# A gated mix of a state-space model and a feed-forward block: parameter rows on another queue, the decay from a tanh

## The chip, the cores and the metric

The kernel runs on one core of a Trainium2 chip. The metric is the device time of one execution in microseconds (us), less is better. A core has TensorE (PE, matrix products into PSUM banks), VectorE (DVE), ScalarE (ACT), GpSimd (POOL) and SyncE (SP), each with its own instruction stream in order, and 16 DMA engines that several queues feed. DMAs can be issued from the streams of SP, ScalarE and GpSimd.

## What is computed

```python
def _A_ref(x, ...):                       # state-space model, P = D = 640 complex states
    dt = exp(log_dt);  Lam_bar = exp(dt * Lam)          # Lam = Lambda_re + 1j * Lambda_im
    B_bar = ((Lam_bar - 1.0) / Lam)[:, None] * Bmat
    Bu = einsum("bld,pd->blp", x, B_bar)
    h_t = Lam_bar * h_{t-1} + Bu_t                      # over 2048 tokens
    return 2.0 * einsum("blp,dp->bld", h, Cmat).real + x * Dskip
def _B_ref(x, w1, b1, w2, b2):            # feed-forward, F = 1728
    return gelu_tanh(x @ w1 + b1) @ w2 + b2
g = sigmoid((x * gate_w).sum(-1, keepdims=True))
out = g * _A_ref(x) + (1 - g) * _B_ref(x)
```

x is 1 x 2048 x 640, all inputs and the output are bf16.

## The kernel before, in words

The 2048 tokens are cut into four chunks of 512, the 640 features and the 640 states into five tiles of 128, the 1728 hidden units into thirteen tiles of 128 and a last one of 64. For each chunk there are four stages: `ff1` (x times w1, a GELU on ScalarE), `ssm` (x times B on TensorE, copied to bf16 by ScalarE, then the recurrence on VectorE), `fin_b` (the hidden layer times w2) and `fin_a` (the states times C, added to a seed x * Dskip that VectorE writes into the PSUM bank, gated by VectorE into an output tile `ot` and stored).

The complex recurrence is done without complex multiplications inside the scan. With a decay r = exp(dt * Lambda_re) and an angle, VectorE multiplies Bu by tables of cosines and sines (TCOS, TSIN), runs two real scans with the factor r (line 497), and multiplies back (lines 482 to 521). The tables are made in the first 27 us: a matrix product with the identity (line 372) turns the parameter rows collected in `prmA` (log_dt, Lambda_im, Lambda_re; five rows of 128 each) into columns `colA`; ScalarE takes dt = exp(log_dt) (line 374) and r = exp(dt * Lambda_re) (line 378); VectorE makes the angles `u` for 64 positions and five special ones kept in `tf`, reduces them, and ScalarE takes sines and cosines (386, 388). VectorE then doubles the tables twice (`double`, lines 406 to 420), and lines 422 to 428 write the upper half. A second matrix of rows, `prmB` (gate_w and b1), is turned in the same way at line 391 into `colB`, which holds the GELU's biases.

The order on TensorE, VectorE and ScalarE is the order of the program: the lines from 195 on are scheduled by hand, with an estimate of each engine's clock (`ck`) that decides between which matmuls a VectorE step of the recurrence is let out (`let_out`, `dve_now`). The order on SP and GpSimd is that of the program too. The DMAs issued by SP and ScalarE take one of eight completion semaphores in turn; a DMA waits until the one eight places ahead of it has landed.

At the start, SP issues the first tokens (line 136), two transposing loads of the rest of chunk 0's features (`load_turned`, line 151), then weights; the tokens' first two feature tiles are turned on TensorE instead (`turn_first`). ScalarE's queue issues three of the w1 tiles and two parameter rows. GpSimd makes the identity, an index row and constants, and issues no DMA:

```python
    load_turned(0)
    rows(nc.sync, prmA[2 * KS:3 * KS, :], A_Lambda_re)
    rows(nc.scalar, prmA[0:KS, :], A_log_dt)
    rows(nc.scalar, prmA[KS:2 * KS, :], A_Lambda_im)
    load_turned(H)
```

TensorE meanwhile multiplies whatever has arrived: `part(kd, a)` takes feature tile kd of token tile a, `strip` several token tiles, for six hidden tiles in six banks. The turn of `prmA` stands between `part(0, 3)` and `part(1, 3)`, that of `prmB` after the third hidden tile of the last strip. On VectorE the copy of `colB` (line 392) stands ahead of everything that makes the tables out of the sines (418 on).

Later, `load_xn` loads the untransposed tokens of a chunk for the seeds; those of chunk 3 are loaded in halves, the others whole. Output tiles have two buffers, so the third waits for the first one's store.

Of the kernel before, what the change touches and what calls it, by code (L numbers as in the profile page):

```python
# [10 lines left out]
ALU = mybir.AluOpType  # L11
ACT = mybir.ActivationFunctionType
BF16 = mybir.dt.bfloat16
F32 = mybir.dt.float32
I32 = mybir.dt.int32

P = 128
T = 2048
D = 640
# [4 lines left out]
KS = D // P  # L24
KF = (F + P - 1) // P
F_LAST = F - (KF - 1) * P
NT = T // P
TPC = CH // P
H = TPC // 2
# [12 lines left out]
def kernel(  # L42
# [19 lines left out]
    nc = tc.nc  # L62
# [4 lines left out]
    const = ctx.enter_context(tc.tile_pool(name="const", bufs=1))  # L67
# [7 lines left out]
    def bank(dtype=F32):  # L75
        return ps.tile([P, CH * 4 // (4 if dtype == F32 else 2)], dtype, name="bank")
# [18 lines left out]
    ident = const.tile([P, P], BF16, name="ident")  # L95
    prmA = const.tile([P, P], BF16, name="prmA")
    NB = KS + KF - 1
    prmB = const.tile([P, P], BF16, name="prmB")
    colA = const.tile([P, 3 * KS], F32, name="colA")
    colB = const.tile([P, NB], F32, name="colB")  # L100
    Dbc = const.tile([P, D], BF16, name="Dbc")
    glast = const.tile([P, 2, KS], F32, name="glast")
    carry = const.tile([P, 2, KS], F32, name="carry")
# [9 lines left out]

    ldt_c = colA[:, 0:KS]
    lim_c = colA[:, KS:2 * KS]
    lre_c = colA[:, 2 * KS:3 * KS]
    b1_c = colB[:, KS:NB]


    def load_xn(c, a0=0, a1=TPC, queue=None):  # L120
        if a0 == 0:
            xn[c] = xnp.tile([P, TPC, D], BF16, name="xn")
        r0 = c * CH + a0 * P
        (queue or nc.sync).dma_start(out=xn[c][:, a0:a1, :], in_=x2d[r0:r0 + (a1 - a0) * P, :].rearrange("(a p) d -> p a d", p=P))
# [4 lines left out]
    def rows(queue, dst, v):  # L129
        queue.dma_start(out=dst, in_=v.rearrange("(j p) -> j p", p=P))  # L130

    KA = 2
    xn[0] = xnp.tile([P, TPC, D], BF16, name="xn")

    def load_x0(queue, a0, a1, d0, d1):
        queue.dma_start(out=xn[0][:, a0:a1, d0:d1], in_=x2d[a0 * P:a1 * P, d0:d1].rearrange("(a p) d -> p a d", p=P))
# [13 lines left out]
    def load_turned(a):  # L150
        nc.sync.dma_start_transpose(out=xT[0][:, KA:KD, a * P:(a + H) * P], in_=x2d[a * P:(a + H) * P, KA * P:D])

    load_turned(0)
    rows(nc.sync, prmA[2 * KS:3 * KS, :], A_Lambda_re)
    rows(nc.scalar, prmA[0:KS, :], A_log_dt)
    rows(nc.scalar, prmA[KS:2 * KS, :], A_Lambda_im)
    load_turned(H)
    load_w1a(nc.sync, 4)
    load_w1a(nc.sync, 3)
    for kd in range(KD):  # L160
        if kd == 1:
            rows(nc.sync, prmB[KS:NB, :], B_b1[0:(KF - 1) * P])
            rows(nc.sync, prmB[0:KS, :], gate_w)
        nc.sync.dma_start(out=w1b[kd][:], in_=B_w1[kd * P:(kd + 1) * P, cut1:cut2])
    for t, k0, k1 in ((w1c_lo, 0, 3), (w1c_hi, 3, KD)):
        nc.sync.dma_start(out=t[:, :, 0:F - cut2], in_=B_w1[k0 * P:k1 * P, cut2:F].rearrange("(k p) f -> p k f", p=P))
# [1 line left out]
    HC = CH // 8  # L168
    tfi = work.tile([P, HC], I32, name="e")
    nc.gpsimd.iota(tfi[:], pattern=[[1, HC]], base=0, channel_multiplier=0)  # L170
    nc.gpsimd.memset(b1x[:, F_LAST:F_LAST + 1], 0.0)
    NQ = 5
    NP = NQ + HC
# [7 lines left out]
    nc.sync.dma_start_transpose(out=xT[1][:], in_=x2d[CH:2 * CH, :])  # L181
    nc.sync.dma_start_transpose(out=CT_re[:], in_=A_C_re[:, :])
    nc.sync.dma_start_transpose(out=CT_im[:], in_=A_C_im[:, :])
    for k0, k1 in ((0, KF - 1),):
        nc.sync.dma_start(out=w2_sb[:, k0:k1, :], in_=B_w2[k0 * P:k1 * P, :].rearrange("(kf p) d -> p kf d", p=P))
    for h in range(2):
        nc.sync.dma_start(out=w2l[h * F_LAST:(h + 1) * F_LAST, :], in_=B_w2[(KF - 1) * P:F, :])
    load_x0(nc.sync, 0, TPC, KA * P, D)
    nc.sync.dma_start(out=b2bc[:], in_=B_b2.rearrange("(o d) -> o d", o=1).to_broadcast([P, D]))
    nc.sync.dma_start(out=Dbc[:], in_=A_Dskip.rearrange("(o d) -> o d", o=1).to_broadcast([P, D]))  # L190
    nc.sync.dma_start_transpose(out=xT[2][:], in_=x2d[2 * CH:3 * CH, :])
    nc.sync.dma_start_transpose(out=xT[3][:], in_=x2d[3 * CH:4 * CH, :])
    load_xn(1)

    ctx.enter_context(tc.manual_schedule(engines={E.PE, E.DVE, E.Activation}))

# [1 line left out]
    class Clock:  # L198
        pe = 3.4
        act = 12.0  # L200
# [26 lines left out]
    def act(cost):  # L227
        ck.act = max(ck.act, ck.pe + 0.2) + cost
        return ck.act
# [5 lines left out]
    pA = bank()  # L235
# [24 lines left out]
    def col(name, dtype=F32, n=KS):  # L260
        return const.tile([P, n], dtype, name=name)

    dt16 = col("dt16", BF16)
    dtl = col("dtl")
    limp = col("limp")
    thp_c = col("thp_c")
    r_c = col("r_c")
    hs = [None] * NCH
    gel = [None] * NCH
    gbs = [None] * NT  # L270
    def ff1_mm(p, c, kf, kd, t0=0, t1=CH, first=None, last=KD - 1):
        w, f0 = (w1a, 0) if kf < FA else (w1b, FA) if kf < FB else (w1c, FB)
        w = w[kd][:, (kf - f0) * P:(kf - f0 + 1) * P]
        nc.tensor.matmul(p[:, t0:t1], lhsT=w, rhs=xT[c][:, kd, t0:t1],  # L274
                         start=(kd == 0) if first is None else first, stop=(kd == last), skip_group_check=first is not None)
        pe(t1 - t0)

    def ff1_act(p, c, kf):
        nc.scalar.activation(out=gel[c][:, kf, :], in_=p[:, :], func=ACT.Gelu_apprx_tanh, bias=b1_c[:, kf:kf + 1])  # L279
        act(0.69)  # L280
# [71 lines left out]
    def over(c, n):  # L352
        return c.rearrange("p (k o) -> p k o", o=1).to_broadcast([P, KS, n])
# [15 lines left out]
    part(1, 2)  # L369
    part(0, 3)  # L370
    pP = bank()
    nc.tensor.matmul(pP[:, 0:3 * KS], lhsT=prmA[:], rhs=ident[:, 0:3 * KS], start=True, stop=True, skip_group_check=True)
    nc.vector.tensor_copy(out=colA[:], in_=pP[:, 0:3 * KS])
    nc.scalar.activation(out=dt16[:], in_=ldt_c, func=ACT.Exp)
    nc.vector.tensor_scalar(out=limp[:], in0=lim_c, scalar1=INV_2PI, scalar2=None, op0=ALU.mult)
    nc.vector.tensor_tensor(out=dtl[:], in0=dt16[:], in1=lre_c, op=ALU.mult)
    nc.vector.tensor_tensor(out=thp_c[:], in0=dt16[:], in1=limp[:], op=ALU.mult)
    nc.scalar.activation(out=r_c[:], in_=dtl[:], func=ACT.Exp)
    nc.vector.tensor_tensor(out=u, in0=tf[:].rearrange("p (o i) -> p o i", o=1).to_broadcast([P, KS, NP]), in1=over(thp_c[:], NP), op=ALU.mult)
    part(1, 3)  # L380
    strip(2, 0, HT, False)
# [6 lines left out]
    nc.scalar.activation(out=FSC[:, KS:2 * KS, 0:NP], in_=ab, func=ACT.Sin, scale=-TWO_PI_M, bias=halfpi[:])  # L388
    for kf in range(FA):
        if kf == 3:  # L390
            nc.tensor.matmul(pA[:, 0:NB], lhsT=prmB[:], rhs=ident[:, 0:NB], start=True, stop=True, skip_group_check=True)
            nc.vector.tensor_copy(out=colB[:], in_=pA[:, 0:NB])
        ff1_mm(banks[kf], 0, kf, 3, 0, CH, False, 3)
    for kf in range(FA):
        ff1_act(banks[kf], 0, kf)
# [3 lines left out]
            ff1_mm(two_banks[i], 0, FA + i, kd)  # L399
    for i in range(2):  # L400
        ff1_act(two_banks[i], 0, FA + i)
    for t, k0, k1 in ((w1c_lo, 0, 3), (w1c_hi, 3, KD)):
        nc.gpsimd.tensor_copy(out=t[:, :, n1c - 1:n1c], in_=colB[:, k0:k1].rearrange("p (k o) -> p k o", o=1))
    ff1(0, FA + 2)

    def double(n, i):
        lo, hi = slice(0, n), slice(n, 2 * n)
        s, c = (over(t[:, i * KS:(i + 1) * KS], n) for t in (sq, cq))
        m1, m2 = (scr[:, (3 + j) * KS * P:(3 + j) * KS * P + KS * n].rearrange("p (k i) -> p k i", k=KS) for j in range(2))
        nc.vector.tensor_tensor(out=m1, in0=FC[:, :, lo], in1=c, op=ALU.mult)  # L410
        nc.vector.tensor_tensor(out=m2, in0=FS[:, :, lo], in1=s, op=ALU.mult)
        nc.vector.tensor_tensor(out=FC[:, :, hi], in0=m1, in1=m2, op=ALU.subtract)
        nc.vector.tensor_tensor(out=m1, in0=FC[:, :, lo], in1=s, op=ALU.mult)
        nc.vector.tensor_tensor(out=m2, in0=FS[:, :, lo], in1=c, op=ALU.mult)
        nc.vector.tensor_tensor(out=FS[:, :, hi], in0=m1, in1=m2, op=ALU.add)
# [3 lines left out]
    double(HC, 4)  # L419
    double(2 * HC, 3)  # L420
    nsH = col("nsH")
    nc.vector.tensor_scalar(out=nsH[:], in0=sH, scalar1=-1.0, scalar2=None, op0=ALU.mult)
    for ks in range(KS):
        for dst, X, xs, Y in ((TCOS, FS, nsH, FC), (TSIN, FC, sH, FS)):
# [109 lines left out]
    def ssm(c, at={}):  # L534
        hs[c] = hsp.tile([P, 2 * KS, CH], BF16, name="hs")
        for ks in range(KS):
            if ks in at:
                at[ks]()
            bu = work.tile([P, 2, CH], BF16, name="bu", bufs=8)
            for ri, BT in enumerate((BT_re, BT_im)):  # L540
                p = bank()
                for kd in range(KD):
                    nc.tensor.matmul(p[:], lhsT=BT[ks >= KSA][:, kd, (ks % KSA if ks < KSA else ks - KSA) * P:][:, 0:P], rhs=xT[c][:, kd, :],  # L543
                                     start=(kd == 0), stop=(kd == KD - 1))
                    pe(CH)
                nc.scalar.activation(out=bu[:, ri, :], in_=p[:], func=ACT.Identity)  # L546
                act(0.6)
            scan_ops(c, ks, bu, ck.act)
            if c == 0 and ks == 0:
                later(0, 1.6, factors)  # L550
            let_out(ck.pe)
# [43 lines left out]
    def first_banks(c):  # L595
        biased(c, "wide", 0)
        biased(c, "wide", 1)
# [90 lines left out]
    ff1(2, 0, {1: lambda: fold(3), 4: lambda: fold(4), 9: lambda: seed(0), 11: lambda: seed(1)})  # L688
    gates(2)
    fin_a(0)  # L690
    load_xn(2)
    ssm(2, {KS - 1: lambda: first_banks(1)})
    fin_b(1, seeds(1))
    fin_a(1)
# [41 lines left out]
```

## Time and profile before

| what | value |
|---|---|
| median of 5 runs | 216.05 us (215.59 to 216.78) |
| the profiled execution | 216.31 us, its span 214.5 us |
| granted TensorE clock | 1.00 |
| busy: TensorE, VectorE, ScalarE, GpSimd | 209.1, 188.0, 101.9, 1.8 us |
| DMA | 16.23 MB, mean 76 GB/s |
| idle of TensorE until prmA had landed | 0.5 us |

The span runs from the first instruction to the end of the last. Busy times of engines overlap. In a row of waits, the name on the left waited for the one on the right; in a chain, each piece was released by the one before it. L372 is line 372 of the kernel. The page's slices show how the loads lie: the DMA engines are busy in the first quarter of the span, and little after that.

```profile
DMA  6898999999200000061000006100000000110012
```

Each digit is the busy share in tenths of one of 40 slices of 5.4 us.

### The profile page before, as it was taken

The numbers are of one execution on the slowest core, as the hardware profiler recorded it, in microseconds if no ns is written. First come the engines' busy times: TensorE is split into PE (matmuls) and PEld (weight loads), VectorE is DVE, ScalarE is ACT, GpSimd is POOL, SyncE is SP. The second block draws the span as 40 slices with busy tenths as digits, with TensorE's granted clock in tenths as the row PEclk, the third lists the DMA queues.
The fourth block names the chain that finished last, engine by engine and source line by source line (L and its number), as shares of the span: only waits on it lengthen the run. The fifth ranks groups of instructions, "written<-read, shape, count | busy, mean of one in ns | idle before, by whom it ended". The sixth has DMA issues, their size and how long they took to land.

```text
span 214.5 us, 3528 instructions
## 1 busy us (share of the span) xinstructions
PE 209.1 (97%) x1372; PEld 125.1 (58%) x1383; DVE 188.0 (88%) x381; ACT 101.9 (47%) x182; POOL 1.8 (1%) x15
## 2 busy tenths in 40 slices
PE   8899999999999999999999999999999989999994
PEld 5745444454576644774456777444457567676773
DVE  2589999999989999998999999799999999995153
ACT  3599856665868588203653210456691421405100
POOL 1001000000000000000000000000000000000000
PEclk9999999999999999999999999999999999999999
DMA  6898999999200000061000006100000000110012
GB/s 185 208 172 184 226 176 219 355 248 200 67 0 0 3 0 0 14 184 63 0 0 3 0 0 176 42 29 0 2 5 12 0 3 0 61 64 0 0 63 64
DMA packets 33139, 16.23 MB, mean 76 GB/s; under 512 B 24546, under 2 KB 33122, under 8 KB 33122
## 3 DMA queue, kind: packets, MB, share of 16 engines
q1 hardware_dynamic: 32526, 15.38, 30.6%
q10 hardware_dynamic: 596, 0.63, 0.9%
q8 instruction: 11, 0.18, 0.4%
q14 instruction: 6, 0.05, 0.1%
HBM read 7.48 MB, written 2.62 MB: 47 GB/s over the span
## 4 chain that ended last, share of the span: by engine, by line
DVE 70%; PE 20%; DMA 5%; issue 2%; ACT 1%; ACTq 0%; DVEq 0%
DVE g L497 19%; PE bank L661 10%; DVE wa L478 10%; DVE wb L478 10%; PE bank L602 7%; DVE v L478 6%; DVE hs L478 6%; DMA out_dram<-ot 4%; DVE bank L576 3%; DVE ot L666 3%; PE bank L274 2%; DVE CT_re L466 2%; DVE CT_im L466 2%; DMA prmA<-in_A_Lambda_im_dram 1%; DVE g L426 1%
## 5 line engine op out<-in xcount | busy, mean ns | idle before, releaser
L602 PE MATMUL bank<-w_sb,gel 128*128 128x384 bf16 (+1 forms) x416 | 57.9, 299 | 0.0
L602 PEld LDWEIGHTS <-gel 128*128 128x128 bf16 x416 | 40.3, 98 | 17.0 <-issue 0.8
L546 ACT ACTIVATE bu<-bank 128x512 bf16<-128x512 f32 x40 | 23.6, 597 | 37.3 <-PE bank L543 37.2
L279 ACT ACTIVATE gel<-bank,colB 128x512 bf16<-128x512 f32 x52 | 33.9, 692 | 11.1 <-PE bank L274 10.8
L661 PEld LDWEIGHTS <-hs 128*128 128x128 bf16 x330 | 31.7, 98 | 12.5 <-issue 0.8
L497 DVE TENSOR_TENSOR_SCAN g<-r_c,carry,v 128x512 bf16<-128x512 f32 x30 | 37.2, 1271 | 0.0
L610 ACT ACTIVATE gb<-bank,gcol 128x384 f32<-128x384 f32 (+1 forms) x32 | 15.1, 526 | 32.1 <-PE bank L602 16.9
L666 DVE SCALAR_TENSOR_TENSOR ot<-bank,gcol,gb 128x320 bf16<-128x320 f32 (+2 forms) x33 | 17.6, 535 | 12.2 <-PE bank L661 9.5
L661 PE MATMUL bank<-CT_re,hs 128*128 128x320 bf16 (+2 forms) x165 | 27.1, 295 | 0.6 <-DVE bank L576 0.6
L274 PE MATMUL bank<-xT,w1a 128*128 128x512 bf16 (+2 forms) x158 | 27.2, 324 | 0.2
L661 PE MATMUL bank<-CT_im,hs 128*128 128x320 bf16 (+2 forms) x165 | 27.1, 295 | 0.0
L543 PE MATMUL bank<-xT,BT_im 128*128 128x512 bf16 x99 | 24.8, 379 | 0.1
L543 PE MATMUL bank<-xT,BT_re 128*128 128x512 bf16 x97 | 24.5, 379 | 0.2
L274 PEld LDWEIGHTS <-w1a 128*128 128x128 bf16 x162 | 14.0, 99 | 11.8
L274 PE MATMUL bank<-xT,w1b 128*128 128x512 bf16 x80 | 18.1, 379 | 0.2 <-DMA w1b<-in_B_w_dram 0.2
L543 PEld LDWEIGHTS <-BT_im 128*128 128x128 bf16 x100 | 9.8, 98 | 11.8
L591 ACT ACTIVATE bank<-b2bc 128x384 f32<-128x384 bf16 (+1 forms) x24 | 11.7, 529 | 9.7 <-DVE ot L666 9.7
L543 PEld LDWEIGHTS <-BT_re 128*128 128x128 bf16 x100 | 9.7, 98 | 11.0
L478 DVE TENSOR_TENSOR v<-wa,wb 128x512 bf16<-128x512 bf16 x40 | 15.2, 422 | 0.6
L576 DVE TENSOR_TENSOR bank<-xn,Dbc 128x320 f32<-128x320 bf16 (+2 forms) x33 | 14.4, 483 | 1.0 <-ACT gb L610 0.9
L478 DVE TENSOR_TENSOR wa<-TCOS,g 128x1024 bf16<-128x1024 bf16 x20 | 13.7, 686 | 0.1
L478 DVE TENSOR_TENSOR wb<-TSIN,bu 128x1024 bf16<-128x1024 bf16 x20 | 13.7, 685 | 0.0
(103 smaller groups left out, 167.7 us busy)
## 6 DMA issues: line engine op xcount, KB each, us to landing
out_dram<-ot SPq DMA_DIRECT2D x15, 160.0 KB, 1.8
w_sb<-in_B_w_dram SPq DMA_DIRECT2D x1, 2080.0 KB
xn<-in_A_x_dram SPq DMA_DIRECT2D x2, 640.0 KB, 4.2
w1b<-in_B_w_dram SPq DMA_DIRECT2D x5, 128.0 KB, 3.1
xn<-in_A_x_dram SPq DMA_DIRECT2D x2, 320.0 KB, 3.7
w1a<-in_B_w_dram ACTq DMA_DIRECT2D x3, 192.0 KB, 3.8
w1a<-in_B_w_dram SPq DMA_DIRECT2D x2, 192.0 KB, 3.3
xn<-in_A_x_dram SPq DMA_DIRECT2D x1, 384.0 KB
```

The source lines that it names most:

```text
L274: nc.tensor.matmul(p[:, t0:t1], lhsT=w, rhs=xT[c][:, kd, t0:t1], start=(kd == 0) if first is None else first, stop=(kd == last), skip_grou ...
L279: nc.scalar.activation(out=gel[c][:, kf, :], in_=p[:, :], func=ACT.Gelu_apprx_tanh, bias=b1_c[:, kf:kf + 1])
L478: nc.vector.tensor_tensor(out=o, in0=a, in1=b, op=op)
L497: nc.vector.tensor_tensor_scan(s["g"][:, ri, :], r_c[:, ks:ks + 1].to_broadcast([P, CH]), s["v"][:, ri, :], init, ALU.mult, ALU.add)
L543: nc.tensor.matmul(p[:], lhsT=BT[ks >= KSA][:, kd, (ks % KSA if ks < KSA else ks - KSA) * P:][:, 0:P], rhs=xT[c][:, kd, :], start=(kd == 0 ...
L546: nc.scalar.activation(out=bu[:, ri, :], in_=p[:], func=ACT.Identity)
L576: dve_now(ck.pe, 0.45, lambda: nc.vector.tensor_tensor(out=p[:, 0:d1 - d0], in0=xn[c][:, a, d0:d1], in1=Dbc[:, d0:d1], op=ALU.mult))
L591: nc.scalar.activation(out=v, in_=src, func=ACT.Identity)
L602: nc.tensor.matmul(p[:, col:col + d1 - d0], lhsT=gel[c][:, kf, a * P:(a + 1) * P], rhs=w2_sb[:, kf, d0:d1], start=False, stop=False, skip_ ...
L610: nc.scalar.activation(out=gbs[ti][:, d0:d1], in_=p[:, col:col + d1 - d0], func=ACT.Identity, scale=gcol[:, 1, ti:ti + 1])
L661: nc.tensor.matmul(p[:, 0:d1 - d0], lhsT=hs[c][:, j, lo:lo + P], rhs=CT[:, j % KS, d0:d1], start=False, stop=(j == 2 * KS - 1), skip_group ...
L666: nc.vector.scalar_tensor_tensor(out=ot[:, d0:d1], in0=p[:, 0:d1 - d0], scalar=gcol[:, 0, ti:ti + 1], in1=gbs[ti][:, d0:d1], op0=ALU.mult, ...
```

## The change

All five parameter and bias rows are issued by GpSimd, behind its iota and its identity and ahead of the constants of `tf`. Lambda_re moves from `prmA` to `prmB`, so `prmA` is turned with ten columns and `prmB` with 23. As Lambda_re is now known only after `prmB` has been turned, the product dt * Lambda_re moves behind the copy of `colB`, and the decay is no longer taken with ScalarE's Exp but from a tanh between two GELUs: with t = tanh(z / 2), exp(z) = (1 + t) / (1 - t), made by four VectorE instructions ahead of `nsH`. The two transposing loads of the first chunk follow each other in SP's queue. w2 is loaded in three parts instead of one, and the untransposed tokens of chunks 0 (the later features), 1 and 2 in halves. The orders of VectorE's, ScalarE's and TensorE's other instructions stay as they were.

```diff
-    rows(nc.sync, prmA[2 * KS:3 * KS, :], A_Lambda_re)
-    rows(nc.scalar, prmA[0:KS, :], A_log_dt)
-    rows(nc.scalar, prmA[KS:2 * KS, :], A_Lambda_im)
     load_turned(H)
...
     for kd in range(KD):
-        if kd == 1:
-            rows(nc.sync, prmB[KS:NB, :], B_b1[0:(KF - 1) * P])
-            rows(nc.sync, prmB[0:KS, :], gate_w)
         nc.sync.dma_start(out=w1b[kd][:], in_=B_w1[kd * P:(kd + 1) * P, cut1:cut2])
...
     nc.gpsimd.iota(tfi[:], pattern=[[1, HC]], base=0, channel_multiplier=0)
+    rows(nc.gpsimd, prmA[0:KS, :], A_log_dt)
+    rows(nc.gpsimd, prmA[KS:2 * KS, :], A_Lambda_im)
+    rows(nc.gpsimd, prmB[KS:NB, :], B_b1[0:(KF - 1) * P])
+    rows(nc.gpsimd, prmB[NB:NB + KS, :], A_Lambda_re)
+    rows(nc.gpsimd, prmB[0:KS, :], gate_w)
     nc.gpsimd.memset(b1x[:, F_LAST:F_LAST + 1], 0.0)
...
-    for k0, k1 in ((0, KF - 1),):
+    for k0, k1 in ((0, 4), (4, 8), (8, KF - 1)):
         nc.sync.dma_start(out=w2_sb[:, k0:k1, :], ...)
...
-    load_x0(nc.sync, 0, TPC, KA * P, D)
+    load_x0(nc.sync, 0, H, KA * P, D)
+    load_x0(nc.sync, H, TPC, KA * P, D)
...
-    load_xn(1)
+    load_xn(1, 0, H)
+    load_xn(1, H, TPC)
...
-    nc.vector.tensor_tensor(out=dtl[:], in0=dt16[:], in1=lre_c, op=ALU.mult)
     nc.vector.tensor_tensor(out=thp_c[:], in0=dt16[:], in1=limp[:], op=ALU.mult)
-    nc.scalar.activation(out=r_c[:], in_=dtl[:], func=ACT.Exp)
...
-            nc.vector.tensor_copy(out=colB[:], in_=pA[:, 0:NB])
+            nc.vector.tensor_copy(out=colB[:], in_=pA[:, 0:NB + KS])
+            nc.vector.tensor_tensor(out=dtl[:], in0=dt16[:], in1=lre_c, op=ALU.mult)
...
     for i in range(2):
         ff1_act(two_banks[i], 0, FA + i)
+    nc.scalar.activation(out=thr[:], in_=dtl[:], func=ACT.Tanh, scale=0.5)
+    act(0.2)
...
+    nc.vector.tensor_scalar(out=rden[:], in0=thr[:], scalar1=-1.0, scalar2=1.0, op0=ALU.mult, op1=ALU.add)
+    nc.vector.reciprocal(out=rden[:], in_=rden[:])
+    nc.vector.tensor_scalar(out=thr[:], in0=thr[:], scalar1=1.0, scalar2=None, op0=ALU.add)
+    nc.vector.tensor_tensor(out=r_c[:], in0=thr[:], in1=rden[:], op=ALU.mult)
     nc.vector.tensor_scalar(out=nsH[:], in0=sH, scalar1=-1.0, scalar2=None, op0=ALU.mult)
...
-    load_xn(2)
+    load_xn(2, 0, H)
+    load_xn(2, H, TPC)
```

## The prediction, made before the changed kernel was run

> **What bounds the kernel now.** I read the page's busy times first, then the chain that ended last, then the waits of TensorE and VectorE.
>
> ```profile
> PE 209.1 (97%) x1372; PEld 125.1 (58%) x1383; DVE 188.0 (88%) x381; ACT 101.9 (47%) x182; POOL 1.8 (1%) x15
> DVE 70%; PE 20%; DMA 5%; issue 2%; ACT 1%; ACTq 0%; DVEq 0%
> ```
>
> TensorE is busy 97% of the span, yet 70% of the chain lies on VectorE. The waits tell which of the two decides. First TensorE's over the whole span, then VectorE's between 11.5 and 174.9 us (who <- for whom: us, times, longest):
>
> ```profile
> PE bank L661 <- DVE bank L576: 0.6, 1, 0.6
> PE bank L372 <- DMA prmA<-in_A_Lambda_im_dram: 0.5, 1, 0.5
> PE bank L274 <- DMA w1b<-in_B_w_dram: 0.2, 1, 0.2
> ```
>
> ```profile
> DVE ot L666 <- DMA out_dram<-ot: 2.6, 2, 1.5
> DVE CT_re L466 <- ACT ft L462: 1.0, 1, 1.0
> DVE colB L392 <- PE bank L391: 0.8, 1, 0.8
> ```
>
> After its copy of colB VectorE never waits for TensorE until 174.9 us; its three later waits are for things that it released itself (an output tile's store, a fold's factor). TensorE waits for VectorE once, and there the end is set (the chain, start and length):
>
> ```profile
> 174.43 0.42 DVE bank L576
> 174.85 0.04 issue
> 174.89 1.11 PE bank L661 x7
> ```
>
> From 174.89 TensorE works without a wait to the end. So the time is: when VectorE begins its long run (11.5 us), plus that run, plus a fixed TensorE tail. TensorE has 0.62 us to spare at 174.89. A stall taken from TensorE alone buys nothing; it counts as far as it starts VectorE's run earlier. What starts that run is the chain between 7 and 13 us:
>
> ```profile
> 4.52 3.04 DMA prmA<-in_A_Lambda_im_dram
> 7.55 0.14 issue
> 7.69 0.17 PE bank L372
> 7.86 1.66 PE bank L274 x18
> ...
> 11.53 0.18 DVE colB L392
> 11.71 0.09 DVE sq L418
> ```
>
> The Lambda_im row lands at 7.55, TensorE turns prmA at 7.69 and goes on in order to prmB at 11.30; VectorE copies colB at 11.53 and only then may begin the doubling (sq at 11.63). The second sine (10.73 + 0.59 = 11.32) is ready just before.
>
> **The change part by part.** *Rows moved.* The two prmA rows leave ScalarE's queue (3.89 and 4.52) for GpSimd's, which is free after the affine select, 1.10 + 0.29 = 1.39. No row here shows a DMA issued by GpSimd. The same kind of row costs 0.27 to 0.59 us to issue on the other queues; the longest plain copy issued without a transfer ahead of it that stops the queue is b2bc's on SP, 1.45. I take 0.59, the longest of the same rows. From the start of its issue to landing, Lambda_im took 3.04. The second row starts at 1.39 + 0.59 = 1.98 and has landed by about 5.0 (at 1.45 each: 2.84 and 5.9). TensorE needs it at 7.0: its eighteen 128-column matmuls start at 6.00 and are 0.056 apart ((1.17 - 0.22)/17), so the next could start at 7.01. The wait of 0.52 goes; by starts the gain is up to 7.69 - 7.01 = 0.68.
>
> *What is late next* on TensorE is w1a[4], issued on SP at 5.79, landing after at most 3.4 (9.2), used at about 9.4. Without Lambda_re in SP's queue (4.04 to 4.54) the second transpose and w1a[4] are issued 0.5 earlier: 8.7, where TensorE now wants it at 8.7. So I count **0.6** of the 0.68. The second transpose follows the first with only a semaphore of w1a[0], which TensorE was already using at 4.05. The two prmB rows leave SP too (7.32 to 8.14, against a usual gap of 0.05), so w1b[1] to w1b[4] go out about 1.3 earlier; the w1b wait of 0.2 goes or at worst stays, on an engine with slack.
>
> *prmB* now takes three rows, issued third to fifth. The last starts at 1.39 + 4 x 0.59 = 3.75; gate_w, issued at 7.81, had landed when TensorE loaded prmB at 11.09, so 3.3 at most: 7.1 (at 1.45: 7.19 and 10.5); needed at about 10.5. The constants of tf are written on GpSimd after these DMAs: ready at 1.39 + 5 x 0.59 + 0.3 = 4.6 instead of 1.6, used by u at 8.69 - 0.6 - 0.09 = 8.0. At 1.45 they are ready at 8.9, u starts at 8.95, 0.26 later than before, and the second sine ends at 11.58.
>
> The Trainium skill, "DMA: Bandwidth & Descriptors", section "Latency and other measured facts", gives about 1 us to the first byte from GpSimd's queue against about 0.6 from the others; by it the fifth row is issued at about 6.4, still ahead of 8.0, and the sum does not move. The page "SBUF — State Buffer", section "SBUF: two separate sides", speaks against the change: GpSimd cannot write descriptors while VectorE runs certain copies. VectorE's timeline shows five casts of 0.29 us between 3.70 and 6.44; held through all of them the rows would be some 1.5 us later, again without moving the sum.
>
> *VectorE's run.* colB comes 0.6 earlier (10.93). Behind it stands a new multiply for dtl that needs colB, then sq. The factors show what such 5-element operations cost (VectorE's timeline, start and length):
>
> ```profile
> 34.46 0.16 DVE L437 TENSOR_TENSOR q<-colA 128x5 f32<-128x5 f32 x1
> 34.65 0.17 DVE L437 TENSOR_TENSOR den<-den,q 128x5 f32<-128x5 f32 x1
> 34.85 0.19 DVE L445 RECIPROCAL den<-den 128x5 f32<-128x5 f32 x1
> 35.08 0.17 DVE L446 TENSOR_SCALAR den<-den 128x5 f32<-128x5 f32 x1
> 35.16 0.16 DVE L437 TENSOR_TENSOR q<-a_c,colA 128x5 f32<-128x5 f32 x1
> ```
>
> One that needs its predecessor starts 0.20 after it, one that doesn't 0.08. dtl then sq: 0.20 + 0.08 against 0.10 now, **+0.18**; sq at 11.2, the second sine then ended at about 10.7. The old dtl disappears from ahead of thp (0.09, off this path). Before nsH stand four new ones: rden, reciprocal (+0.20), thr + 1 (+0.10), the product r_c (+0.20), then nsH (+0.08): **+0.58**. Their input, a tanh behind the eighth GELU (about 16.6), is ready 2 us before. From 19.6 on everything to 174.43 is VectorE's own run, so nothing hides these.
>
> *ScalarE.* An Exp of 0.21 goes, a tanh goes in between two GELUs (the gate's took 0.17, with no table load). TensorE never waits for ScalarE here; without that cover it would be 0.17.
>
> *Other splits.* w2 in three, xn0, xn1 and xn2 in halves: the same bytes. The transposes of xT[2] and xT[3] now wait for w2's parts, but the DMA share is 0 from 59 us and xT[2] is first used at 71.75; that is the cover. xn2 lies beside the output stores and is a rival below.
>
> **Sum.** VectorE's run starts 0.6 earlier and is 0.18 + 0.58 = 0.76 longer: **+0.16**. With the whole 0.68 it is +0.08; with GpSimd at 1.45 per DMA, sq is held to 11.65, +0.02 + 0.58 = +0.6. The profiled execution took 216.31, its span 214.5 and 1.8 around it; it becomes 216.47. That execution lay 0.26 above the median 216.05, so I forecast 216.2 (216.1 to 216.65).
>
> **Rivals.** (1) *GpSimd's queue becomes the bound.* The tf constants and the prmB rows stand behind five issues. At SP's 1.70 for a transpose (BT_im), constants come at 1.39 + 8.5 + 0.3 = 10.2; u starts 1.5 late, the second sine ends at 12.8, sq at 12.87: 1.24 + 0.58 = +1.8, **217.9**. It decides from 1.41 us an issue (tf ready at 8.7, a shift of 0.65). For it: five in a row on an engine that shows none. Against: the same rows take at most 0.59 elsewhere, and 3.3 us of slack.
>
> (2) *Halving xn2 delays an output store.* VectorE waits 1.05 at 98.19 for a store behind the undivided xn2 and 1.50 at 136.39 behind the halved xn3. From the load's issue to the end of the wait: 92.22 to 98.19, 5.97; 129.91 to 136.39, 6.48. If the halves are the reason, 0.5 more in VectorE's run: +0.66, **216.7**. Against: bytes and order are the same.
>
> (3) *Faster: those same store waits shrink.* They are 2.55 of pure VectorE idleness. If the first goes (1.05), 216.05 + 0.16 - 1.05 = **215.2**; TensorE's slack of 0.62 plus its 0.6 would allow it. Against: nothing in the change takes bytes from ahead of that store.
>
> **Chances.** Forecast 0.47, queue 0.20, halves 0.22, store waits 0.11. This kernel's runs can tell about 0.3%, 0.65 us, from no change. Slower by more: the queue, 0.13 of the halves, 0.03 of the forecast's upper edge: 0.36. Faster: 0.11. Within: 0.53. The range, 215.4 to 218.2, leaves out the faster case and the queue's costs beyond some 1.8 us an issue, which I take for less than half of its 0.20: under 2 in 10.
>
> **What would show it.** Right: TensorE turns prmA near 7.0 without a wait, colB near 10.9, sq near 11.2, nsH near 19.8, and TensorE's wait at L576's bank grows from 0.6 to about 1.4. Wrong: VectorE waiting for tf or for prmB's matmul, GpSimd issuing at over 1.4 us each, or a store wait other than 1.05 and 1.50. The forecast fails as a whole if VectorE's run is not stiff, that is, if it idles somewhere new or idles less.

## The result, and the profile after

| | kernel before | changed kernel |
|---|---|---|
| median (lowest to highest) | 216.05 us (215.48 to 216.94, 43 runs) | 217.57 us (215.95 to 220.05, 24 runs) |
| ratio, 95% interval | 1 | 1.0057 (1.0041 to 1.0072) |
| the profiled execution, its span | 216.31, 214.53 us | 217.19, 215.41 us |

The change made the kernel slower by 0.57%, 1.23 us. (The ratio leaves the three slowest of the 24 executions out and the median counts all, which is part of why the medians lie further apart.) The forecast was 216.2, the range 215.4 to 218.2: the time is inside, but it is a loss and not the "no difference" that was held likeliest.

The page of the changed kernel, busy times and the chain:

```profile
PE 209.8 (97%) x1372; PEld 125.9 (58%) x1383; DVE 188.5 (88%) x385; ACT 101.1 (47%) x182; POOL 4.3 (2%) x20
PE 80%; DVE 18%; issue 1%
```

The chain has turned from 70% VectorE to 80% TensorE, and that is misleading. The waits of TensorE and of VectorE say why:

```profile
PE bank L669 <- DVE bank L584: 1.5, 1, 1.5
```

```profile
DVE ot L674 <- PE bank L551: 1.2, 1, 1.2
DVE ot L674 <- DMA out_dram<-ot: 1.2, 1, 1.2
```

TensorE now waits 1.5 us (1.46) for the seed that VectorE writes for token tile 8, seed(8) from here on, where it waited 0.62, so VectorE decides more than before. VectorE's second wait for a store, at 137.23, is put down to TensorE's L551, because a matmul group happened to end at that moment (137.19). The store issued at 132.56 had landed at 137.14, and the same instruction waited for that store in the kernel before. By this one name in the waits the whole chain ahead of that moment was put down to the other engine. The end itself (the changed kernel's chain):

```profile
175.26 0.42 DVE bank L584
175.68 0.04 issue
175.72 11.10 PE bank L669 x80
```

seed(8) starts at 175.18 (174.34 before), and TensorE goes on from 175.72 (174.89), 0.83 later. The front, on VectorE (start, length; in brackets the idle time before it). nsH is the first operation behind the four that make the decay:

```profile
11.75 0.18 DVE L392 COPY colB<-bank 128x23 f32<-128x23 f32 x1 [0.85 <-PE bank L391]
11.97 0.17 DVE L393 TENSOR_TENSOR dtl<-dt,colB 128x5 f32<-128x5 bf16 x1
12.05 0.18 DVE L421 COPY sq<-hs 128x25 f32<-128x25 f32 x1
```

```profile
20.05 0.17 DVE L426 TENSOR_SCALAR rden<-thr 128x5 f32<-128x5 f32 x1
20.25 0.19 DVE L427 RECIPROCAL rden<-rden 128x5 f32<-128x5 f32 x1
20.36 0.13 DVE L428 TENSOR_SCALAR thr<-thr 128x5 f32<-128x5 f32 x1
20.52 0.17 DVE L429 TENSOR_TENSOR r_c<-thr,rden 128x5 f32<-128x5 f32 x1
20.60 0.16 DVE L430 TENSOR_SCALAR nsH<-sq 128x5 f32<-128x5 f32 x1
```

From colB to nsH it is 8.85 us, 8.09 before: 0.76 more, as forecast. But colB is copied at 11.75, 0.22 later than before and not 0.6 earlier. And yet the waits that were to go did go: TensorE waits for no row any more. GpSimd did what was assumed of it (its timeline):

```profile
1.47 0.65 POOL L130 DMA_DIRECT2D prmA<-in_A_log_dt_dram  x1
2.11 0.52 POOL L130 DMA_DIRECT2D prmA<-in_A_Lambda_im_dram  x1
...
3.64 0.52 POOL L130 DMA_DIRECT2D prmB<-in_gate_w_dram  x1
```

The rows landed between 5.25 and 7.48. TensorE itself was late. Here are two stretches of 1 us, first before, then after (the stretch and its length; busy time and number of instructions of PE, PEld, which is TensorE's weight load, DVE, ACT and POOL; clock, DMA share, GB/s):

```profile
5.00:6.00 1.00, 1.00 (x20) 0.98 (x18) 0.29 (x1) 0.39 (x2) 0.00 (x0) 1.00 0.78 134
6.00:7.00 1.00, 1.00 (x21) 0.99 (x18) 0.29 (x1) 0.28 (x1) 0.00 (x0) 1.00 0.78 132
```

```profile
5.00:6.00 1.00, 1.00 (x12) 0.86 (x10) 0.06 (x1) 0.15 (x1) 0.00 (x0) 1.00 1.28 130
6.00:7.00 1.00, 1.00 (x17) 1.00 (x16) 0.29 (x1) 0.28 (x1) 0.00 (x0) 1.00 1.33 247
```

Twelve matmuls against twenty in the same microsecond. Two things are late. The third and fourth token tiles landed at 5.63 and 6.43 (4.91 and 5.74 before), and TensorE's 128-column matmuls started 0.107 apart until 6.39 and 0.056 apart from then on, which is called full clock below; before, that step came at 4.55. (The clock column says 1.00 throughout, since the trace's clock records only begin with that step.) prmA was turned at 7.91, not 7.0.

### The profile page after: what moved, and what is told of

Its sections match the earlier page's. It is cut to its first block, busy times and chain, and to the rows that moved or that the text cites. A ratio compares the mean times of both kernels' runs of the same rounds, so it can differ in the third digit from the quotient of the medians.

```text
span 215.4 us, 3540 instructions
## 1 busy us (share of the span) xinstructions
PE 209.8 (97%) x1372; PEld 125.9 (58%) x1383; DVE 188.5 (88%) x385; ACT 101.1 (47%) x182; POOL 4.3 (2%) x20
## 3 DMA queue, kind: packets, MB, share of 16 engines
HBM read 7.48 MB, written 2.62 MB: 47 GB/s over the span
## 4 chain that ended last, share of the span: by engine, by line
PE 80%; DVE 18%; issue 1%
PE bank L669 20%; PE bank L276 20%; PE bank L610 20%; PE bank L551 16%; DVE g L505 6%; DVE wa L486 3%; DVE wb L486 3%; DVE hs L486 2%; DVE v L486 2%; PE bank L238 1%; PE bank L626 1%; PE bank L302 1%; DVE ot L674 1%; PE bank L241 0%; DVE bank L584 0%
## 5 line engine op out<-in xcount | busy, mean ns | idle before, releaser
L276 PE MATMUL bank<-xT,w1a 128*128 128x512 bf16 (+2 forms) x158 | 27.8, 332 | 0.2
L551 PE MATMUL bank<-xT,BT_im 128*128 128x512 bf16 x99 | 24.8, 379 | 0.1
L551 PE MATMUL bank<-xT,BT_re 128*128 128x512 bf16 x97 | 24.5, 379 | 0.2
L276 PEld LDWEIGHTS <-w1a 128*128 128x128 bf16 x162 | 14.8, 103 | 11.7
L551 PEld LDWEIGHTS <-BT_im 128*128 128x128 bf16 x100 | 9.8, 98 | 11.8
L551 PEld LDWEIGHTS <-BT_re 128*128 128x128 bf16 x100 | 9.6, 98 | 11.0
```

## The experiments

After this profile two theories stood for the late front. **Q**: GpSimd's five row loads run beside the token loads and hold them up. **C**: TensorE's full clock comes at a moment that differs from execution to execution, and the kernel before hid this behind its wait for a row. For the loss as a whole, **V** stood against **F**: V, VectorE's five added operations are the cost; F, they hide and the rows and splits cost.

**1. The changed kernel again**, no edit.

> The changed kernel once more, nothing edited. Its first profile had VectorE's run begin 0.42 us later instead of 0.42 earlier, because TensorE reached prmA's turn at 7.91 and not at 7.0: the third token tile was turned at 5.67 (before: 5.05), and matmuls of 128 columns stayed 0.107 us apart until 6.40 (before: until 4.54). Theory Q (GpSimd's rows delay the token loads): third and fourth token tile again turned near 5.7 and 6.8, prmA at 7.6 to 7.9, median about 217.5. Theory C (nothing is delayed, the moment at which TensorE's clock opens varies from execution to execution, and the old kernel hid it behind its wait for prmA): token tiles anywhere between 5.05 and 5.7, prmA's turn anywhere between 7.0 and 7.9, single times from 216.0 to 218.

217.6 (216.92 to 218.13), ratio 1.0071 (1.0047 to 1.0095). The loss repeats. In the profile full clock came at 4.21, prmA was turned at 7.60, and VectorE waited 2.75 for stores in place of 2.40. So neither prmA's time nor the store waits are properties of the kernel; the 8.85 from colB to nsH is.

**2. The rows back on SP's and ScalarE's queues**, the rest as changed.

```diff
+    rows(nc.sync, prmB[NB:NB + KS, :], A_Lambda_re)
+    rows(nc.scalar, prmA[0:KS, :], A_log_dt)
+    rows(nc.scalar, prmA[KS:2 * KS, :], A_Lambda_im)
     load_turned(H)
...
+            rows(nc.sync, prmB[KS:NB, :], B_b1[0:(KF - 1) * P])
+            rows(nc.sync, prmB[0:KS, :], gate_w)
...
-    rows(nc.gpsimd, prmA[0:KS, :], A_log_dt)
...
-    rows(nc.gpsimd, prmB[0:KS, :], gate_w)
```

> The changed kernel with the five rows back on SP's and ScalarE's queues, where the kernel before had them; the tanh, the four VectorE steps and the halved loads stay. Theory Q: token tiles turned at 5.05 and 5.9 again, prmA's turn waits for its rows until about 7.6, colB near 11.5, VectorE's run 0.76 longer: 216.8. Theory C: the same time, 216.8, but token tiles need not be earlier. If the rows in GpSimd's queue cost nothing at all, 217.5, as the changed kernel.

217.48 (216.76 to 219.5), ratio 1.0072 (1.0044 to 1.01). Still slow, with prmA turned at 8.00: the fourth token tile landed at 5.44, as early as ever, but full clock came at 6.75. In this profile C alone made TensorE this late, and GpSimd's queue is not the main cost.

**3. The rows alone by GpSimd**: the kernel before, with its Exp and no split; Lambda_re stays in prmA.

```diff
-    rows(nc.sync, prmA[2 * KS:3 * KS, :], A_Lambda_re)
...
     nc.gpsimd.iota(tfi[:], pattern=[[1, HC]], base=0, channel_multiplier=0)
...
+    rows(nc.gpsimd, prmA[2 * KS:3 * KS, :], A_Lambda_re)
+    rows(nc.gpsimd, prmB[KS:NB, :], B_b1[0:(KF - 1) * P])
+    rows(nc.gpsimd, prmB[0:KS, :], gate_w)
```

> The kernel before with only the rows moved: all five by GpSimd, Lambda_re still in prmA, the Exp kept, no tanh, no halved loads. Theory Q: tokens late, prmA's turn at 7.6 to 7.9 and so no earlier than before, 216.0 to 216.3. Theory C: half of the executions gain 0.6 (215.4), half nothing; median about 215.7 with a spread of 1 us. If the 0.76 of VectorE's added steps is wrong and the queue alone made the loss, 217.3.

217.65 (216.01 to 218.26), ratio 1.0065 (1.0043 to 1.0086): as slow as the whole change. This looked like a refutation of V, but the trace shows otherwise. nsH starts at 19.41, 0.21 earlier than before, and the last store is issued at 212.25 against 212.18. Of the 1.27 us that the span grew, 1.20 lie after the last store's issue. SP's waits near the end, before and then here:

```profile
SPq L731 <- DMA out_dram<-ot: 1.4, 2, 1.2
```

```profile
SPq L730 <- DMA out_dram<-ot: 2.4, 2, 1.3
```

Three pieces add up to it in this profile. The last of that store's sixteen completions came 0.79 after the one before it (214.55, 213.76): its last packets moved only from 213.82, when an 8 KB instruction fetch of 0.57 had ended, and the others were through by 213.38. In the kernel before that fetch came at 208.53. With five fewer DMAs on SP's and ScalarE's queues, that store's semaphore came second in the list of waits that ends the kernel instead of last, so five waits of 0.065 each followed it, 0.33. GpSimd's drains and its clearing of the semaphores took 0.08 longer. In the changed kernel, which has as many DMAs there as the kernel before, the first two are absent, and its end is only 0.05 longer. Run 6 puts this to the test.

**4. The rows later**: four GpSimd memsets of 0.98 us; they stand ahead of all five rows in the program, but ran between them, so the order on GpSimd is not always the program's (row issues at 2.28, 3.81, 5.21, 6.61, 7.12).

```diff
+    pad = const.tile([P, 1024], F32, name="pad")
+    for _ in range(4):
+        nc.gpsimd.memset(pad[:], 0.0)
     rows(nc.gpsimd, prmA[0:KS, :], A_log_dt)
```

> The changed kernel with four memsets of an unused 128 x 1024 tile on GpSimd ahead of its five rows, so that the rows are issued after the token loads. One look, for the start alone. Theory Q: token tiles turned at 5.05 and 5.9, TensorE reaches prmA at about 7.0 and waits for rows that land at 8 or later. Theory C: tokens as late as in the changed kernel, or anywhere between.

One execution, 220.27. The fourth token tile landed at 5.45, although the second transposing load goes out as early as in the changed kernel (3.98, 3.97), which speaks for Q; full clock came at 6.15 all the same and prmA was turned at 7.82, which speaks for C. The rest of this run's lateness is something else. Its VectorE waited 1.66 and 2.42 for stores, and what TensorE's waits and its clock then show is this (windows as above; the clock is the number before the last two):

```profile
PE bank L672 <- DVE bank L587: 3.0, 2, 2.7
```

```profile
174.00:177.00 3.00, 0.64 (x6) 0.41 (x5) 2.93 (x7) 0.84 (x2) 0.00 (x0) 0.97 0.00 0
177.00:180.00 3.00, 2.69 (x11) 1.50 (x11) 2.97 (x8) 0.00 (x0) 0.00 (x0) 0.50 0.03 5
180.00:184.00 4.00, 4.00 (x30) 2.84 (x29) 4.00 (x8) 0.35 (x1) 0.00 (x0) 0.97 0.00 0
```

TensorE's wait of 2.67 us for seed(8) began at 174.64. Its clock stood at half from 176.82, 2.18 into that wait, to 180.23, and from seed(8) to the last store it took 39.19 instead of 37.84.

**5. The decay alone**: the kernel before with the tanh; Lambda_re's row is issued at its old place, into prmB.

```diff
-    rows(nc.sync, prmA[2 * KS:3 * KS, :], A_Lambda_re)
+    rows(nc.sync, prmB[NB:NB + KS, :], A_Lambda_re)
...
-    nc.scalar.activation(out=r_c[:], in_=dtl[:], func=ACT.Exp)
...
+            nc.vector.tensor_tensor(out=dtl[:], in0=dt16[:], in1=lre_c, op=ALU.mult)
...
+    nc.scalar.activation(out=thr[:], in_=dtl[:], func=ACT.Tanh, scale=0.5)
...
+    nc.vector.tensor_tensor(out=r_c[:], in0=thr[:], in1=rden[:], op=ALU.mult)
```

> The kernel before with the decay by a tanh alone: the Lambda_re row goes into prmB but is issued at its old place, and every row stays on the queue it had; no load is split. Theory V (the loss is VectorE's five added operations, 0.18 before sq and 0.58 before nsH): sq about 0.18 and nsH about 0.76 later than before (20.4), seed(8) 0.7 to 0.9 later (175.1 to 175.2), time 216.7 to 216.9. Theory F (the decay hides, and what costs lies with the rows on GpSimd's queue and the splits): time within 0.2 of before, 215.8 to 216.2, even if nsH is later.

216.67 (216.3 to 220.16), ratio 1.0043 (1.0021 to 1.0064), that is +0.93 us (0.45 to 1.38). As V expects. colB to nsH is 8.85. Its TensorE shows the same late seed:

```profile
PE bank L668 <- DVE bank L583: 1.3, 1, 1.3
```

**6. The decay undone**: the changed kernel with the Exp; the rows on GpSimd and the splits stay.

```diff
+    rows(nc.gpsimd, prmA[2 * KS:3 * KS, :], A_Lambda_re)
-    rows(nc.gpsimd, prmB[NB:NB + KS, :], A_Lambda_re)
...
+    nc.scalar.activation(out=r_c[:], in_=dtl[:], func=ACT.Exp)
...
-    nc.scalar.activation(out=thr[:], in_=dtl[:], func=ACT.Tanh, scale=0.5)
...
-    nc.vector.tensor_tensor(out=r_c[:], in0=thr[:], in1=rden[:], op=ALU.mult)
```

> The changed kernel with the decay undone: Lambda_re back in prmA (its row by GpSimd too), the product and the exponential where they were before, none of the four VectorE operations before nsH. Rows on GpSimd's queue and all splits stay. Theory V: nsH no later than before (19.4 to 19.7), seed(8) at most 0.1 later than 174.34, time 215.7 to 216.3, so over 1.2 below the changed kernel. Theory F: 217.0 or more, little below the changed kernel. In the run with the rows alone the end after the last store was 1.2 longer; if that came from the place of that store's semaphore among the waits that end the kernel and from an instruction fetch beside it, it is gone here, since this kernel issues as many DMAs on SP's and ACT's queues as the kernel before; if GpSimd's queue as such lengthens the end, it stays.

215.84 (214.79 to 216.69, and one execution at 246.01), ratio 0.9989 (0.9968 to 1.001). The loss is gone. Rows by GpSimd and splits together are worth nothing that these runs can tell from zero (-0.69 to +0.22 us), and the longer end of run 3 is gone as well (2.40 from the last store's issue). F falls. TensorE's wait for the seed is nearly as long as in the changed kernel all the same:

```profile
PE bank L662 <- DVE bank L577: 1.4, 1, 1.4
```

**7. The splits alone** on the kernel before (w2, the second part of x0, xn1 and xn2).

```diff
-    for k0, k1 in ((0, KF - 1),):
+    for k0, k1 in ((0, 4), (4, 8), (8, KF - 1)):
...
-    load_xn(1)
+    load_xn(1, 0, H)
+    load_xn(1, H, TPC)
```

> The kernel before with the splits alone: w2 in three loads, the second part of x0 and the tiles xn1 and xn2 in halves, nothing else. Theory V: VectorE's run unchanged to within 0.2 up to the first wait for a store at 98, waits for stores together 2.0 to 3.2, time 215.9 to 216.4 (0.2 of it from three more waits in the list that ends the kernel). Rival of the prediction (halves delay the store that VectorE waits for): the waits for stores 0.5 longer than before's 2.55, the landing of the stores issued at 94.3 and 131.4 later than 3.8 and 4.9, time 216.5 or more.

215.92 (215.36 to 216.73), ratio 1.0005 (0.9987 to 1.0024). Store waits 1.26 and 0.75, together less than before's 2.55. The prediction's second rival falls.

**8. The decay shared with GpSimd**: only the reciprocal stays on VectorE.

```diff
-            nc.vector.tensor_tensor(out=dtl[:], ...)
+            nc.gpsimd.tensor_tensor(out=dtl[:], ...)
...
+    nc.gpsimd.tensor_scalar(out=rden[:], in0=thr[:], scalar1=-1.0, scalar2=1.0, ...)
+    nc.gpsimd.tensor_scalar(out=thr[:], in0=thr[:], scalar1=1.0, ...)
...
+    nc.gpsimd.tensor_tensor(out=r_c[:], in0=thr[:], in1=rden[:], op=ALU.mult)
```

> The changed kernel with four of the five added operations of the decay on GpSimd (the product dtl, 1-thr, 1+thr and the last product); VectorE keeps the reciprocal alone, 0.2. Theory V: nsH 0.5 to 0.6 earlier than in the changed kernel (about 20.0), time 0.5 to 0.9 below the changed kernel's 217.6, 216.7 to 217.1. Theory F: as the changed kernel, 217.3 to 217.8. If the reciprocal waits for GpSimd, VectorE shows a wait for GpSimd at 20, and nsH moves back by it.

215.75 (215.1 to 217.71), ratio 1.0 (0.9973 to 1.0026). The loss is gone, rather more than V expected; the interval reaches about 0.6 us either way. From colB to nsH it is 8.20 in place of 8.85 (VectorE's timeline):

```profile
21.71 0.18 DVE L428 RECIPROCAL rden<-rden 128x5 f32<-128x5 f32 x1
21.81 0.13 DVE L430 TENSOR_SCALAR nsH<-sq 128x5 f32<-128x5 f32 x1
```

The reciprocal costs 0.10 here and waits for nobody. (Both start late because in this one profile full clock came only at 9.67, and prmA was turned at 9.76. It was the slowest of the twelve executions.) The tanh itself, and its place beside the GELUs, cost nothing that this run can tell.

**9 to 11. Four output tiles instead of two**, in the kernel before, in the changed kernel, and in the kernel of run 6. VectorE then has no store to wait for.

```diff
-            ot = fwork.tile([P, D], BF16, name="ot", bufs=2)
+            ot = fwork.tile([P, D], BF16, name="ot", bufs=4)
```

> The kernel before with four output tiles in place of two, so that VectorE no longer waits for a store to land. Theory V (the end is set by VectorE's run, which is fixed work plus its two waits for stores, and behind it by TensorE, which has 0.6 in hand): the waits at 98 and 136 are gone, seed(8) some 2.0 to 2.6 earlier (about 172), TensorE's wait of 0.62 at 175 is gone and nothing more comes of it, as TensorE is then the bound: span about 213.9, time 215.2 to 215.6. Rival W (the loss of the changed kernel lies in its front or at its end, and VectorE's run only follows): time within 0.2 of before.

> The changed kernel with four output tiles in place of two. Theory V: VectorE's added 0.76 stays (nsH still about 20.4), but seed(8) is 1.2 to 2.4 earlier than 175.18, before TensorE needs it; TensorE's wait of 1.5 at 175 is gone, and with it the runs in which the clock falls there (219 to 220): the time is TensorE's own, 215.3 to 216.0, no more than 0.3 above the kernel before with four tiles. Rival W: the loss stays, 217.0 or more.

> The changed kernel with the decay by its exponential again, as in the earlier run, and four output tiles. Theory V: as the changed kernel with four tiles to within 0.3 (215.2 to 215.9), since VectorE's 0.76 no longer reaches the end. Rival W: 0.5 or more below the changed kernel with four tiles, as it was with two.

| with four output tiles | median | ratio to before | seed(8) | span |
|---|---|---|---|---|
| before | 215.27 (214.69 to 216.44) | 0.9972 (0.9955 to 0.999) | 171.99 | 213.76 |
| changed | 215.42 (214.82 to 215.99) | 0.9972 (0.9955 to 0.9988) | 172.72 | 213.87 |
| Exp back | 215.32 (214.76 to 215.84) | 0.9965 (0.9948 to 0.9982) | 171.33 | 213.14 |

This decides it for V. With the store waits gone TensorE never waits for VectorE, and the change costs 0.15 us by the medians, nothing by the ratios. The changed kernel with four tiles, chain and TensorE's waits:

```profile
PE 95%; DMA 2%; SPq 1%; issue 0%; DVE 0%
```

```profile
PE bank L238 <- PEq L729: 0.8, 1, 0.8
PE bank L241 <- DMA xn<-in_A_x_dram: 0.7, 2, 0.5
```

Both waits left lie in the first microseconds. All three are faster than the kernel before, by 0.60 to 0.76 us; the 0.6 that TensorE had in hand is what could be won.

**12. The decay with its four operations twice**, on the kernel of run 5; nothing uses the second four.

```diff
+    nc.vector.tensor_scalar(out=rd2[:], in0=r_c[:], scalar1=-1.0, scalar2=3.0, ...)
+    nc.vector.reciprocal(out=rd2[:], in_=rd2[:])
+    nc.vector.tensor_scalar(out=thr[:], ...)
+    nc.vector.tensor_tensor(out=thr[:], in0=thr[:], in1=rd2[:], op=ALU.mult)
     nc.vector.tensor_scalar(out=nsH[:], in0=sH, scalar1=-1.0, ...)
```

> The kernel before with the decay by a tanh, as in the run with the decay alone, and four more VectorE operations of the same kinds and size behind the four, whose results nothing uses: VectorE's added time 0.18 + 0.58 + 0.58 = 1.34 in place of 0.76. Theory V with a slope of one: nsH about 1.2 to 1.4 later than 19.62, time 0.5 to 0.7 above the decay alone's 216.67, 217.1 to 217.5. Theory V+C (VectorE's lateness costs more than its own length, because TensorE's wait for seed(8), 2.0 here, lets its clock fall to half for some 3.4 us in some runs): a third of the runs or more at 219 to 220.5 with a mean granted clock of 0.991 to 0.992, where the decay alone had 2 of 12. Without VectorE as the cause: as the decay alone, 216.5 to 216.9.

217.07 (217.01 to 217.65), ratio 1.0061 (1.0041 to 1.0081). colB to nsH is 9.52, 0.67 more than in run 5, and the time is 0.40 more by the medians. The sign is as V expects, but the intervals of runs 5 and 12 overlap, so the cost for each microsecond of VectorE is not pinned down. None of the six executions shows the fallen clock. That lateness is multiplied through the clock is thus not supported, though six executions are too few to rule it out, at two in twelve in run 5.

## Why the prediction was right or wrong

One sum closes to 0.01 us for every profile with two output tiles: nsH, the two store waits and the last three columns ahead of the span add up to the span. VectorE's run from nsH to seed(8), less its two waits for stores, is the same to 0.04 us; so is the stretch from seed(8) to the last store's issue, but for the fallen clock of run 4 (us; all from VectorE's timeline, TensorE's turn of prmA and the last store's issue):

| kernel | prmA | nsH | colB to nsH | store waits | nsH to seed(8), less waits | seed(8) to last store | end | span |
|---|---|---|---|---|---|---|---|---|
| before | 7.69 | 19.62 | 8.09 | 1.05 + 1.50 | 152.17 | 37.84 | 2.35 | 214.53 |
| changed | 7.91 | 20.60 | 8.85 | 1.20 + 1.20 | 152.17 | 37.84 | 2.40 | 215.41 |
| changed, again | 7.60 | 20.30 | 8.85 | 0.90 + 1.85 | 152.17 | 37.84 | 2.40 | 215.46 |
| rows back | 8.00 | 20.70 | 8.85 | 0.80 + 1.69 | 152.18 | 37.83 | 2.53 | 215.73 |
| rows alone | 7.24 | 19.41 | 8.09 | 1.01 + 1.81 | 152.18 | 37.84 | 3.55 | 215.80 |
| rows later | 7.82 | 20.52 | 8.85 | 1.66 + 2.42 | 152.16 | 39.19 | 2.41 | 218.37 |
| decay alone | 7.30 | 20.22 | 8.85 | 1.25 + 1.06 | 152.18 | 37.84 | 2.35 | 214.90 |
| decay twice | 7.28 | 20.65 | 9.52 | 1.16 + 1.14 | 152.17 | 37.83 | 2.33 | 215.29 |
| decay undone | 7.46 | 19.60 | 8.09 | 1.45 + 1.46 | 152.18 | 37.84 | 2.40 | 214.92 |
| splits alone | 7.59 | 19.52 | 8.09 | 1.26 + 0.75 | 152.17 | 37.84 | 2.53 | 214.07 |
| decay shared | 9.76 | 21.81 | 8.20 | 0.76 + 0.97 | 152.14 | 37.83 | 2.41 | 215.92 |

- **VectorE's run sets the end, and it is stiff**: right, to hundredths of a microsecond, and shown from the other side by the four output tiles.
- **VectorE's run 0.76 longer**: right, 8.85 against 8.09. Runs 5, 6 and 8 show that the loss comes with it and goes with it.
- **The run starts 0.6 earlier**: wrong, and this is the step that failed. It measured 0.22 later in the profile of the changed kernel. The wait of 0.52 for the row did go, although the Lambda_im row landed at 6.36 and not at 5.0. But the step took TensorE's own arrival, 7.01, from one execution as if it were fixed. prmA was turned at 7.24 to 9.76 in the seven profiles with rows early on GpSimd (run 10's 8.12 and run 11's 7.50 included; median 7.60), and at 7.28 to 8.16 in the six with rows on the other queues (run 9's 8.16 included; median 7.64). No gain is left. Q is one reason: the fourth token tile landed at 6.06 to 6.95 in those seven, at 5.43 to 5.98 in those six, and at 5.45 when GpSimd issued late. C is another: full clock came at 3.47 to 9.67 in the one group and at 3.85 to 6.75 in the other (run 10's trace has no clock record). How the lateness divides between the two was not measured. Nor does an early prmA reach VectorE whole: of the four profiles that turned it before 7.5, three took 3.81 to 3.84 from there to prmB's turn, where every other profile took 3.61 or 3.62; in run 5 TensorE waited 0.28 there for w1a[4], which the prediction had named as next.
- **The sum**: +0.16 was made of -0.60 and +0.76. In the profiles it was +0.22 for the front, +0.76 for the run, -0.15 for the store waits (2.40 for 2.55) and +0.05 for the end, together the +0.88 of the span.
- **Store waits of 1.05 and 1.50 as constants**: wrong. Between 1.73 and 4.08 together, with no edit that touches them in run 1. The stores land behind the token loads issued just ahead of them: the one that ends the first wait took 3.5 to 4.4 us from issue to landing, the one of the second 4.1 to 5.8, and other stores 1.8. They may make up much of the spread of the times, which no run shows; that they moved was the sign named for a failing forecast.
- **TensorE's wait at the seed grows from 0.6 to 1.4**: 1.46, right by luck. By the forecast's terms TensorE would have been 0.6 earlier and VectorE 0.16 later. TensorE reached the seed at 174.26 (174.27 before), and VectorE was 0.84 later. Run 6, without the decay, has 1.38, so the sign could not tell.
- **The range**: that the time lies in it is luck too. The forecast's own terms ended at 216.65; the room above was left above all for rival 1, which did not happen.
- **GpSimd's queue as the bound (rival 1)**: 0.52 to 0.65 an issue (0.76 at most, in run 8), no wait for tf or prmB; it falls. **Halves (rival 2)** fall by run 7. **Shorter store waits (rival 3)** were not the change's doing, but four output tiles realized the 0.6 that it named as TensorE's slack.

The Trainium skill, "DMA: Bandwidth & Descriptors", section "Queues, rings and completion order", says that a DMA engine takes packets from its queues in turn; the later fourth tile beside a third busy queue fits that. The skill's "TensorE: Matmul & The Clock Gate", "Part 1: The HAM clock gate", calls the moment of full clock run-variable, and the 3.47 to 9.67 measured here agree, though they spread wider than the page's ±500 ns; that speaks against taking 7.01 as fixed. The page puts the window that decides at 3413 ns and asks for an idle window of about that length before the clock falls. Run 4's half clock lasted 3.41 us, but it began 2.18 into a wait of 2.67, sooner than the page asks for.

What stays open: the changed kernel's 1.23 us (0.89 to 1.56) is more than the decay alone (0.93), less what run 6 shows for the rest (-0.24); the intervals overlap, and no profile shows a further cost. In the same way run 8 took 1.23 off by moving 0.65 away from VectorE, and run 12 lost only 0.40 by 0.67 more; that VectorE's operations are the cause is shown, the price of each microsecond is not. Why the clock falls in a few executions was not settled either: four of 24 of the changed kernel, one of run 2 and two of run 5 have a mean clock of 0.991 to 0.992 as run 4 has, none of run 12.

## What to carry to other kernels

A stall that the profile shows on an engine is a gain only up to that engine's next arrival, and at the start of a kernel that arrival depends on loads and on a clock that differ between executions; do not book it from one trace. Tiny VectorE operations lengthen the run that sets the end, here by 0.76 us for five of 5 elements a partition, so put them on an idle engine. Where two engines end close together, first see what the later one idles for: two more output tiles won 0.6 us and made the whole question of this change idle.

## What the runs showed of the hardware that was not expected

- A DMA queue that runs beside the others has a price for them: with GpSimd's five rows in flight, 0.01 MB, the fourth token tile landed some 0.9 us later (medians 6.43 and 5.49), and at 5.45 in run 4, where the rows went out later.
- The end of a kernel is not constant: 2.33 to 2.53 us from the last store's issue to the last instruction, and 3.55 in run 3, where an instruction fetch held up the last store's packets and that store's semaphore stood early in the list of closing waits. An experiment that changes the number of DMAs can show a difference that has nothing to do with its purpose.
- TensorE's clock fell to half 2.18 us into a wait of 2.67 and stayed there for 3.41 us (run 4); waits of up to 1.85 (run 1) did not bring it down in the profiles.
- On GpSimd a TENSOR_SCALAR of 128x5 took 0.64 to 0.70 us and a TENSOR_TENSOR 0.20 to 0.34 (run 8), against 0.13 to 0.17 on VectorE; off the path they cost nothing that run 8 could tell.
